# Tiled matmul groups issued in pairs, values loaded ahead of queries, and new plan times in an attention and MoE kernel

## The chip, the core and the metric

The kernel runs on one core of one Trainium2 chip. The metric is the device time of one execution in microseconds (us); the time before is the median of three runs. TensorE (PE in the profile) multiplies matrices into PSUM; ScalarE (ACT) and VectorE (DVE) evacuate PSUM and do elementwise work; GpSimd (POOL) issues the loads here and SyncE (SP) the transposing DMAs and the stores.

## The reference

For each of 8 batches and 8 heads, 576 tokens with head dimension 64, and 32 packed queries p per head:

```
p_packed = softmax(p k^T / 8) v
out      = softmax(q p_packed^T / 8) p_packed
x = out, heads side by side: 4608 tokens x 512
h = x @ w_in                 (512 x 2048)
g = h where h >= 1, 0 where h <= -1, else (h + 1)^2 / 4
result = g @ w_out           (2048 x 512)
```

## The kernel before, in words

The kernel folds the packed values into the first weight matrix: M = p_packed times the head's rows of w_in (`mk`, lines 472 to 483), so that the hidden layer is M times the second softmax A. A batch has these tasks, each a group of matmuls on TensorE followed by evacuations:

- `trans` (351): k and q, 96 tokens by 128, are transposed in two parts each (kT0, kT1, qT0, qT1). In batches 0 to 2 TensorE does it, and ScalarE or VectorE copies the result out (tile `tp`; in batch 0 as two copies). From batch 3 on (`TURNED`) a DMA of SyncE does it (`turned`, 485).
- `scores` (378): sc0 and sc1, 12 matmuls of 64 columns each, into one PSUM tile `sp`; ScalarE takes the exponential into `ex`.
- `packed` (397): exp times values, and the row sums (tile `pk`, shown as pk); a copy, an add and a copy make `ppT`, a reciprocal makes `rs`.
- `weights` (432), for two groups g of four heads: s2 (tile `s2`, shown as s in the profile, line 439), an exponential on ScalarE (`eT`), sm (sums over keys by a matmul with a block of ones), a logarithm (`ln`) and an exponential (`rc`) on ScalarE for the reciprocal, and the product `A` on VectorE.
- `mk` (472), for four quarters f of the 2048 hidden features: tile `mp`, cast into `M` by ScalarE or VectorE.
- `hidden_tile` (512), 16 per batch: h = M times A, 4 matmuls of 288 columns (line 519), then x on ScalarE (line 524), a second step on either engine (529 or 531), and hT on VectorE (534).
- `out_tile` (555), 9 for each pair of batches: 16 matmuls of 512 columns (line 562) into `o`, a copy to `ob` (line 307) and stores.

s2 and mp are tiled: each of their eight matmuls uses 64 rows and 32 columns of the array, so that the eight lie side by side. All other matmuls use the whole array. Group g of the heads before is h = 2a + g for a in 0 to 3, so each group needs both halves of qT.

PSUM has three wide tiles (`psW`, `NW`=3, of two banks each), used in turn by all tasks but the output tiles, and two output tiles (`psO`). Until the first outputs run, TensorE is kept busy by matmuls on zeros (line 624).

The order on every engine is static. `Plan` simulates the engines with the costs in `C` and emits the instructions in the order that it finds. Each task has a key (its priority), dependences, a PSUM room that it `takes`, and tasks that free the room again. `ready` says when a task can start, `choose` picks by time and key, `run` advances the clocks. `switch` is what it adds whenever TensorE goes between tiled and whole (`mode`), `land` what a DMA takes after its transfer, `xt` and `xland` the time and delay of a transposing DMA. Loads go through GpSimd's queue in the order in which `add_load` and `add_weights` are called: k, q and v of batch 0, w_in and w_out in quarters by turns, k, q and v of batch 1, then p.

Of the kernel before, what the change touches and what calls it, by code (L numbers as in the profile page):

```python
# [11 lines left out]
C = dict(load=3.0, w_in=2.65, w_out=2.55, out=9.0, p=3.1, land=1.9, xt=5.0, xland=2.5,  # L12
         tpp=0.06, tp=0.042, sc=0.034, pk=1.05, s2=0.25, sm=0.245, M=0.345, h=0.49, o=0.217, switch=0.05,
         pTc=0.1, Tca=1.12, Tcd=0.76, Tc2a=0.64, Tc2d=0.457, ex=0.82, ppT=0.42, ppo=0.41, ppa=0.4, ppd=0.2, rs=0.18, eT=0.74, ln=0.65, rc=0.68, A=0.82,
# [7 lines left out]
class Task:  # L22

    def __init__(self, engines, cost, key, deps, fn, takes, readers, frees, mode, slack, after, holds):
        self.engines, self.cost, self.key, self.deps, self.fn = engines, cost, key, list(deps), fn
        self.takes, self.readers, self.frees, self.mode = takes, readers, frees, mode
        self.slack, self.after, self.holds = slack, after, holds
        self.users, self.end, self.slot, self.gone = [], None, None, 0.0


class Plan:
# [24 lines left out]
    def ready(self, t, e):  # L56
        at = 0.0
        for d in t.deps:
            if e == "PE":
                lag = 0.0 if d.on == "PE" else C["feed"] + (C["margin"] if t.slack is None else t.slack)  # L60
            else:
                lag = C["array"] if d.on == "PE" else C["tell"] if d.on != e else 0.0
            at = max(at, d.end + lag)
        if t.takes:
            room = self.rooms[t.takes][self.count[t.takes] % len(self.rooms[t.takes])]
            if room is None:
                return None
            at = max(at, room + (C["feed"] if e == "PE" else 0.0))
        return at
# [39 lines left out]
    def run(self, idle):  # L109
# [10 lines left out]
        n = len(self.tasks)  # L120
        while n:
# [24 lines left out]
            if t.takes:  # L146
                room = self.rooms[t.takes]
                t.slot = self.count[t.takes] % len(room)
                room[t.slot] = None
                self.count[t.takes] += 1  # L150
                if t.readers == 0:
                    room[t.slot] = t.end + t.holds
            if t.frees is not None:
                f = t.frees
                f.gone = max(f.gone, t.end)
                f.readers -= 1
                if f.readers == 0:
                    self.rooms[f.takes][f.slot] = f.gone
# [17 lines left out]
def kernel(  # L176
# [95 lines left out]
    def add_load(nm, b, parts=1, deps=()):  # L272
        for i, hs in enumerate([ALL] if parts == 1 else HS):
            L[nm, b, i] = add(DMA, C["load"] / parts, -1, deps, lambda nm=nm, b=b, hs=hs: load(nm, b, hs))
        if parts == 1:
            L[nm, b, 1] = L[nm, b, 0]
# [62 lines left out]

    def attention(b, key):  # L340
# [9 lines left out]
        def trans(nm, i, dst, prev):  # L350
            box, ky = {}, key[nm + "T" + str(i)]

            def mm():
                tp = box["tp"] = wide([P, X, 1024], bf16, "tp")
                for j in range(X):
                    for h2 in range(2):
                        for e in range(E):
                            o = (h2 * E + e) * TP
                            nc.tensor.transpose(tp[:, j, o:o + TP],  # L359
                                                tok[nm, b][:, 4 * i + 2 * j + h2, X * e:X * (e + 1)].rearrange("p c d -> p (c d)"),  # L360
                                                ident[:TP, :TP])
            split = 2 if b == 0 else 1
            t = add(PE, C["tp"] * 12, ky, [L[nm, b, i]] + prev, mm, takes="W", readers=split, mode=0)
            if split == 1:
                def cp(eng):
                    w = 4 * E * TP
                    copy(dst()[:, i, :w].rearrange("p (j c) -> p j c", j=X), box["tp"][:, :, :w // 2])(eng)
                return t, [both(cp, C["Tca"], C["Tcd"], ky, [t], frees=t)]
            res = []
            for j in range(X):  # L370
                def cp(eng, j=j):
                    w = 2 * E * TP
                    copy(dst()[:, i, j * w:(j + 1) * w], box["tp"][:, j, :w])(eng)
                res.append(both(cp, C["Tc2a"], C["Tc2d"], ky, [t], frees=t))
            return t, res

        def scores(i, deps):
            box, ky = {}, key["sc" + str(i)]

            def mm():  # L380
                sp = box["sp"] = wide([P, 2, FW], f32, "sp")
                for j in range(2):
                    for e in range(E):
                        for g in range(G):
                            h, o = G * (2 * i + j) + g, (e * G + g) * X * NP
                            w = ((G * j + g) * E + e) * TP
                            nc.tensor.matmul(sp[:, j, o:o + X * NP], kT()[:, i, w:w + P],  # L387
                                             pT[:, b, h].rearrange("p x n -> p (x n)"), start=True, stop=True)

            def ev(eng):  # L390
                nc.scalar.activation(ex().rearrange("p e g x a n -> p a (e g x) n")[:, 2 * i:2 * i + 2],  # L391
                                     box["sp"][:TP, :, :E * G * X * NP].rearrange("p j (c n) -> p j c n", n=NP),
                                     AF.Exp, scale=scale)
            t = add(PE, C["sc"] * 12, ky, deps, mm, takes="W", readers=1, mode=0)
            return t, add(ACT, C["ex"], ky, [t] + old("pk"), ev, frees=t)

        def packed(deps):
            box, ky = {}, key["pk"]

            def mm():  # L400
# [3 lines left out]
                for g in range(G):  # L404
                    for a in range(Q):
                        h = G * a + g
# [9 lines left out]
            t = add(PE, C["pk"], ky, [L["v", b, 0]] + deps, mm, takes="W", readers=3, mode=0)  # L416
# [15 lines left out]
        def weights(g, deps, r):  # L432
            box, ky, km = {}, key["s2" + str(g)], key["sm" + str(g)]

            def mm():
                s2 = box["s2"] = wide([P, X, FW], f32, "s2")
                for a in range(Q):
                    for x in range(X):
                        nc.tensor.matmul(s2[a * NP:(a + 1) * NP, x, :HALF], pp_of(x, G * a + g),  # L439
                                         qT()[x * D:(x + 1) * D, a // 2, (G * (a % 2) + g) * E * TP:][:, :E * TP], start=True, stop=True)  # L440
# [21 lines left out]
            t = add(PE, C["s2"], ky, deps, mm, takes="W", readers=1, mode=2)  # L462
            e_ = add(ACT, C["eT"], ky, [t, r] + p_, exp2, frees=t)
# [6 lines left out]
            return t, e_, a_  # L470

        def mk(f, deps):
            box, ky = {}, key["M" + str(f)]

            def mm():
                mp = box["mp"] = wide([P, G, FW], f32, "mp")
                for a in range(Q):
                    for g in range(G):
                        nc.tensor.matmul(mp[a * NP:(a + 1) * NP, g], pp_of(g, G * a + g),  # L479
                                         w_in_sb[g * D:(g + 1) * D, a, f * FW:(f + 1) * FW], start=True, stop=True)  # L480
            t = add(PE, C["M"], ky, deps + [L["in", f]], mm, takes="W", readers=1, mode=2)
            return t, both(lambda eng: copy(M()[:, :, f * FW:(f + 1) * FW], box["mp"])(eng),
                           C["Mca"], C["Mcd"], ky, [t] + K.get((b - 2, "h"), []), frees=t)
# [19 lines left out]
        ws = [weights(g, pc + qc0 + qc1, r) for g in range(G)]  # L503
        ms = [mk(f, pc) for f in range(NF)]
# [50 lines left out]
    def out_tile(pr, i):  # L555
        box, prev = {}, []
        bs = range(2 * pr + i * P // S, 2 * pr + ((i + 1) * P - 1) // S + 1)

        def step(fi):
            if fi == 0:  # L560
                box["o"] = psO.tile([P, d_model], f32, tag="o", name="o")
            nc.tensor.matmul(box["o"], hT[:, fi, i * P:(i + 1) * P], w_out_sb[:, fi, :], start=(fi == 0), stop=(fi == KF - 1))  # L562
# [7 lines left out]
        def done_last(eng):  # L570

            w = d_model // 2
            for j, (eng, queue) in enumerate(((ACT, nc.scalar), (DVE, nc.sync))):
                ob = ops.tile([P, w], f32, tag="ob" + str(j), name="ob" + str(j), bufs=1)
                copy(ob, box["o"][:, j * w:(j + 1) * w])(eng)
                for a, n, dst in out_rows(pr, i):
                    queue.dma_start(dst[:, j * w:(j + 1) * w], ob[a:a + n])
        for fi in range(KF):
# [6 lines left out]
        both(done if 2 * pr + 2 < B or i + 1 < NT else done_last, C["oba"], C["obd"], b_key(pr, i), prev, frees=owner, takes="ob", holds=C["out"])  # L585
# [16 lines left out]
    order = "kT0 qT0 kT1 sc0 qT1 sc1 pk s20 M0 s21 sm0 M1 sm1 M2 M3".split()  # L602
# [52 lines left out]
```

## Time and profile before

| | us |
|---|---|
| median of 3 runs | 260.59 |
| lowest and highest | 259.56, 261.15 |
| the profiled execution, own time | 259.97 |
| its span, first to last instruction | 258.1 |
| TensorE busy | 248.6 |
| ScalarE busy | 189.5 |
| VectorE busy | 176.1 |

A row of the profile reads: start, duration, engine, line, operation, output<-input, shape, count. In a row of groups the numbers behind the bar are the total busy time, the mean of one in ns, and the idle time before with what ended it. Square brackets give an idle time and its releaser. Matmuls are pipelined, so the row of a matmul is longer than its distance to the next: distances between starts tell the cost.

### The profile page before, as it was taken

To read this page: it belongs to the slowest core of one execution; us is meant where nothing else is said; L and a number is where in the kernel's file an instruction comes from. 1 tells how busy PE (TensorE), PEld (TensorE's weight loads), DVE (VectorE), ACT (ScalarE), POOL (GpSimd) and SP (SyncE) were. 2 spreads that over 40 slices of the span, in tenths; PEclk is the share of its full clock that TensorE was granted. 3 is DMA by queue.
4 is the path that set the end of the run, shared out by engine and by line. 5 is a ranking of instruction groups with operands and counts; after the bars stand their busy time and mean duration, and the time that the engine had idled before them with its cause. 6 is when DMAs were issued, how large, how long until landed. Compare 5 with 4: busy or idle time off the path is not lost.

```text
span 258.1 us, 5590 instructions
## 1 busy us (share of the span) xinstructions
PE 248.6 (96%) x2273; PEld 145.2 (56%) x2273; DVE 176.1 (68%) x298; ACT 189.5 (73%) x304; POOL 27.4 (11%) x40
## 2 busy tenths in 40 slices
PE   7999999899999999999999999999999999999992
PEld 5977556357646645654655556555654465644440
DVE  5124997678899988999858885888367877940000
ACT  3438995789899799989869987998669885841110
POOL 8522312102101201110201000000000000000000
PEclk9999999999999999999999999999999999999998
DMA  7999999999999999999999994312021111132223
GB/s 100 181 207 207 206 205 194 218 228 209 164 177 165 164 218 195 166 156 144 181 138 159 214 221 89 79 30 54 4 80 41 43 41 42 43 81 82 60 64 83
DMA packets 54762, 34.38 MB, mean 133 GB/s; under 512 B 27472, under 2 KB 50256, under 8 KB 54736
## 3 DMA queue, kind: packets, MB, share of 16 engines
q0 software_dynamic: 24608, 18.55, 51.0%
q1 hardware_dynamic: 29968, 15.34, 33.8%
q8 instruction: 18, 0.29, 0.4%
q10 hardware_dynamic: 160, 0.13, 0.2%
q14 instruction: 8, 0.07, 0.1%
HBM read 37.22 MB, written 9.44 MB: 181 GB/s over the span
## 4 chain that ended last, share of the span: by engine, by line
PE 76%; DMA 15%; ACT 3%; POOL 2%; issue 1%; DVE 1%; POOLq 0%
PE o L562 45%; PE h L519 21%; DMA p_nat<-in_p_dram 8%; DMA w_out_sb<-in_moe_w_out_dram 7%; PE mp L479 3%; PE sp L387 2%; PE pk L408 2%; PE sm L449 1%; PE s L439 1%; ACT M L307 1%; PE tp L359 1%; PE pk L414 1%; ACT pT L307 1%; POOL w_in_sb L280 1%; ACT eT L444 1%
## 5 line engine op out<-in xcount | busy, mean ns | idle before, releaser
L562 PE MATMUL o<-w_out_sb,hT 128*128 128x512 bf16 x576 | 144.5, 379 | 0.7 <-ACT ob L307 0.5
L534 DVE SCALAR_TENSOR_TENSOR hT<-x 128x576 bf16<-128x576 f32 x128 | 93.3, 754 | 14.0 <-PE o L562 9.8
L562 PEld LDWEIGHTS <-hT 128*128 128x128 bf16 x576 | 54.5, 98 | 56.4 <-issue 5.0
L524 ACT ACTIVATE x<-h 128x576 f32<-128x576 f32 x128 | 78.4, 656 | 9.9 <-PE h L519 6.6
L519 PE MATMUL h<-A,M 128*128 128x288 bf16 x512 | 77.8, 286 | 0.3 <-ACT M L307 0.3
L519 PEld LDWEIGHTS <-M 128*128 128x128 bf16 x512 | 48.4, 98 | 24.7 <-issue 3.0
L529 DVE TENSOR_SCALAR x<-x 128x576 f32<-128x576 f32 x80 | 36.7, 459 | 16.9 <-ACT x L524 16.2
L307 ACT COPY ob<-o 128x512 f32<-128x512 f32 (+1 forms) x22 | 12.7, 577 | 30.8 <-PE o L562 30.7
L531 ACT ACTIVATE x<-x 128x576 f32<-128x576 f32 x48 | 32.1, 683 | 0.7
L307 DVE COPY ob<-o 128x512 f32<-128x512 f32 (+1 forms) x15 | 10.1, 673 | 26.6 <-ACT ob L307 24.9
L307 ACT CAST M<-mp 128x1024 bf16<-128x1024 f32 x20 | 19.9, 1008 | 1.2 <-PE mp L479 1.1
L624 PE MATMUL o<-zeros 128*128 128x256 bf16 x137 | 18.9, 285 | 1.2 <-DVE zeros L242 1.2
L307 DVE CAST M<-mp 128x1024 bf16<-128x1024 f32 x12 | 14.6, 1220 | 1.7 <-PE mp L479 1.6
L624 PEld LDWEIGHTS <-zeros 128*128 128x128 bf16 x137 | 13.4, 102 | 3.5 <-DVE zeros L242 1.2
L460 DVE SCALAR_TENSOR_TENSOR A<-eT,rs,rc 128x576 bf16<-128x576 bf16 x16 | 13.0, 814 | 2.7 <-ACT rc L457 2.6
L391 ACT ACTIVATE ex<-sp 96x768 bf16<-96x768 f32 x16 | 12.9, 814 | 2.0 <-PE sp L387 2.0
L254 POOL DMA_DIRECT2D k<-in_k_dram x9 | 7.3, 812 | 65.9 <-issue 28.0
L444 ACT ACTIVATE eT<-s,rs 128x576 bf16<-128x576 f32 x16 | 11.7, 743 | 2.9 <-PE s L439 2.8
L479 PE MATMUL mp<-w_in_sb,ppT 64*32 64x512 bf16 x256 | 13.1, 384 | 0.5 <-ACT x L524 0.5
L453 ACT ACTIVATE ln<-sm 128x576 f32<-128x576 f32 x16 | 10.5, 655 | 1.6 <-PE sm L449 1.4
L457 ACT ACTIVATE rc<-ln 128x576 f32<-128x576 f32 x16 | 10.9, 683 | 0.5
L387 PEld LDWEIGHTS <-kT 128*128 128x128 bf16 x192 | 7.8, 98 | 2.2 <-ACT kT L307 0.2
(47 smaller groups left out, 114.1 us busy)
## 6 DMA issues: line engine op xcount, KB each, us to landing
q<-in_q_dram POOLq DMA_DIRECT2D x8, 576.0 KB, 14.5
v<-in_v_dram POOLq DMA_DIRECT2D x8, 576.0 KB, 15.0
out_dram<-ob SPq DMA_DIRECT2D x23, 192.0 KB, 3.0
k<-in_k_dram POOLq DMA_DIRECT2D x7, 576.0 KB, 14.1
out_dram<-ob SPq DMA_DIRECT2D x24, 128.0 KB, 2.4
w_in_sb<-in_moe_w_in_dram POOLq DMA_DIRECT2D x4, 512.0 KB, 18.3
w_out_sb<-in_moe_w_out_dram POOLq DMA_DIRECT2D x4, 512.0 KB, 19.0
out_dram<-ob SPq DMA_DIRECT2D x23, 64.0 KB, 2.6
```

What stands on the lines that cost most here:

```text
L307: return lambda eng: nc.vector.tensor_copy(out_, in_) if eng == DVE else nc.scalar.copy(out_, in_)
L387: nc.tensor.matmul(sp[:, j, o:o + X * NP], kT()[:, i, w:w + P], pT[:, b, h].rearrange("p x n -> p (x n)"), start=True, stop=True)
L444: nc.scalar.activation(box["eT"], box["s2"][:, :, :HALF], AF.Exp, scale=rs()[:, g, 1:])
L460: nc.vector.scalar_tensor_tensor(A()[:, g], box["eT"], rs()[:, g, :1], box["rc"], ALU.mult, ALU.mult)
L479: nc.tensor.matmul(mp[a * NP:(a + 1) * NP, g], pp_of(g, G * a + g), w_in_sb[g * D:(g + 1) * D, a, f * FW:(f + 1) * FW], start=True, stop=True)
L519: nc.tensor.matmul(h[:, hf, :HALF], T[b, "M"][:, g, fi * P:(fi + 1) * P], T[b, "A"][:, g, hf], start=(g == 0), stop=(g == G - 1))
L524: nc.scalar.activation(box["x"], box["h"][:, :, :HALF], AF.Prelu, bias=-1.0, alpha=0.5)
L529: nc.vector.tensor_scalar(x, x, 1.0, 0.0, ALU.add, ALU.max)
L531: nc.scalar.activation(x, x, AF.Relu, bias=1.0)
L534: nc.vector.scalar_tensor_tensor(hT[:, fi, col:col + S].rearrange("p (a t) -> p a t", a=2), box["x"], 1.0, box["x"], ALU.min, ALU.mult)
L562: nc.tensor.matmul(box["o"], hT[:, fi, i * P:(i + 1) * P], w_out_sb[:, fi, :], start=(fi == 0), stop=(fi == KF - 1))
L624: plan.run(lambda: nc.tensor.matmul(o[:, :DW], zeros[:, :P], zeros[:, :DW], start=True, stop=True))
```

## The change

- From batch 2 on, s2 of group 0 goes with mp 0, s2 of group 1 with mp 1, and mp 2 with mp 3: each pair is one task of TensorE that takes two wide PSUM tiles. `weights` and `mk` become generators, and `tiled` runs one or two of them. A task can hold several rooms (`slots`, `readers` as a list).
- Head group g is now h = 4g + (a xor g): a half of the heads, so s2 of group g needs qT of half g alone, and the scores task i fills group i. Each score matmul writes its two runs of 32 columns 128 apart, and `ex` is written in one contiguous run per third.
- In batch 0, v is loaded ahead of q, and q in two halves; the copies of kT and qT are one instead of two.
- The last output tile accumulates in two PSUM tiles of 256 columns (one of them a wide one), so each half has its own copy engine; the longer store goes first.
- The plan: `first`=3.8 for the first v and q, `xland` 6.0 for 2.5, `switch` 0.09 on entering tiled work alone, `join` 0.11 off for a pair, `lap` 0.085 by which ScalarE and VectorE overlap successive instructions, the first cast of M on VectorE, more dependences for TensorE's tasks (old readers of `ex`, `ppT`, `A`, `M`), and from batch 1 on both kT ahead of qT.

The diff, cut to its core:

```diff
-C = dict(load=3.0, w_in=2.65, ..., xt=5.0, xland=2.5, ... switch=0.05,
+C = dict(load=3.0, first=3.8, w_in=2.65, ..., xt=5.0, xland=6.0, ... switch=0.09, lap=0.085, join=0.11,
...
         if t.takes:
-            room = self.rooms[t.takes][self.count[t.takes] % len(self.rooms[t.takes])]
-            if room is None:
-                return None
-            at = max(at, room + (C["feed"] if e == "PE" else 0.0))
+            rooms = self.rooms[t.takes]
+            for j in range(len(t.readers)):
+                room = rooms[(self.count[t.takes] + j) % len(rooms)]
+                if room is None:
+                    return None
+                at = max(at, room + (C["feed"] if e == "PE" else 0.0))
...
-                cost += C["switch"]
+                cost += C["switch"] if t.mode else 0.0
                 self.mode = t.mode
-            self.now[e] = at + cost
+            self.now[e] = at + cost - (C["lap"] if e in ("ACT", "DVE") and cost > 0.4 else 0.0)
...
     def first_loads():
         for hs in HS:
             load("k", 0, hs)
+        load("v", 0, ALL)
         make_identity(nc, ident)
...
-    add_load("q", 0)
-    add_load("v", 0)
+    L["v", 0, 0] = L["v", 0, 1] = add(DMA, C["first"], -1, (), lambda: None)
+    add_load("q", 0, 2, cost="first")
...
+    def head(g, a):
+        return 4 * g + (a ^ g)
...
-            split = 2 if b == 0 else 1
...
-                sp = box["sp"] = wide([P, 2, FW], f32, "sp")
-                for j in range(2):
-                    for e in range(E):
-                        for g in range(G):
-                            h, o = G * (2 * i + j) + g, (e * G + g) * X * NP
-                            w = ((G * j + g) * E + e) * TP
-                            nc.tensor.matmul(sp[:, j, o:o + X * NP], kT()[:, i, w:w + P],
-                                             pT[:, b, h].rearrange("p x n -> p (x n)"), start=True, stop=True)
+                sp = wide([P, 1024], f32, "sp")
+                box["sp"] = sp[:TP, :E * X * Q * NP].rearrange("p (e y) -> p e y", e=E)
+                for e in range(E):
+                    o = sp[:, e * X * Q * NP:(e + 1) * X * Q * NP].rearrange("p (x a n) -> p x a n", x=X, a=Q)
+                    for a in range(Q):
+                        h = head(i, a)
+                        w = (h % 4 * E + e) * TP
+                        nc.tensor.matmul(o[:, :, a], kT()[:, i, w:w + P], pT[:, b, h], start=True, stop=True)
...
-                        nc.tensor.matmul(s2[a * NP:(a + 1) * NP, x, :HALF], pp_of(x, G * a + g),
-                                         qT()[x * D:(x + 1) * D, a // 2, (G * (a % 2) + g) * E * TP:][:, :E * TP], start=True, stop=True)
+                        nc.tensor.matmul(s2[a * NP:(a + 1) * NP, x, :HALF], pp_of(x, h),
+                                         qT()[x * D:(x + 1) * D, g, h % 4 * E * TP:][:, :E * TP], start=True, stop=True)
...
-            t = add(PE, C["s2"], ky, deps, mm, takes="W", readers=1, mode=2)
+            t, j = yield ky, C["s2"], deps + p_, mm
...
+        def tiled(*units):
+            units = list(units)
+            asked = [next(u) for u in units]
+            t = add(PE, sum(a[1] for a in asked) - C["join"] * (len(asked) - 1), asked[0][0], [d for a in asked for d in a[2]],
+                    lambda: [a[3]() for a in asked], takes="W", readers=[1] * len(units), mode=2)
+            return [u.send((t, j)) for j, u in enumerate(units)]
...
-        ws = [weights(g, pc + qc0 + qc1, r) for g in range(G)]
-        ms = [mk(f, pc) for f in range(NF)]
+        ws, ms = [weights(g, pc + (qc0, qc1)[g], r) for g in range(G)], [mk(f, pc) for f in range(NF)]
+        if b < 2:
+            ws, ms = [tiled(w)[0] for w in ws], [tiled(m)[0] for m in ms]
+        else:
+            pairs = [tiled(w, m) for w, m in zip(ws, ms)] + [tiled(*ms[2:])]
+            ws, ms = [p_[0] for p_ in pairs[:2]], [p_[1] for p_ in pairs[:2]] + pairs[2]
...
-            nc.tensor.matmul(box["o"], hT[:, fi, i * P:(i + 1) * P], w_out_sb[:, fi, :], start=(fi == 0), stop=(fi == KF - 1))
+            for o, cs in [(box["o"][:, :w], slice(w)), (box["o2"], slice(w, d_model))] if end else [(box["o"], slice(d_model))]:
+                nc.tensor.matmul(o, hT[:, fi, i * P:(i + 1) * P], w_out_sb[:, fi, cs], start=(fi == 0), stop=(fi == KF - 1))
...
-            for j, (eng, queue) in enumerate(((ACT, nc.scalar), (DVE, nc.sync))):
+            for j, (eng, queue, o) in enumerate(((ACT, nc.scalar, box["o"][:, :w]), (DVE, nc.sync, box["o2"]))):
                 ob = ops.tile([P, w], f32, tag="ob" + str(j), name="ob" + str(j), bufs=1)
-                copy(ob, box["o"][:, j * w:(j + 1) * w])(eng)
-                for a, n, dst in out_rows(pr, i):
+                copy(ob, o)(eng)
+                for a, n, dst in sorted(out_rows(pr, i), key=lambda x: -x[1]):
...
-    order = "kT0 qT0 kT1 sc0 qT1 sc1 pk s20 M0 s21 sm0 M1 sm1 M2 M3".split()
+    order = "kT0 kT1 sc0 qT0 sc1 qT1 pk s20 M0 s21 sm0 M1 sm1 M2 M3".split()
```

More of the change, by code (lines that the diff above doesn't have):

```diff
@@ L8 @@
 from concourse._compat import with_exitstack
-C = dict(load=3.0, w_in=2.65, w_out=2.55, out=9.0, p=3.1, land=1.9, xt=5.0, xland=2.5,
-         tpp=0.06, tp=0.042, sc=0.034, pk=1.05, s2=0.25, sm=0.245, M=0.345, h=0.49, o=0.217, switch=0.05,
-         pTc=0.1, Tca=1.12, Tcd=0.76, Tc2a=0.64, Tc2d=0.457, ex=0.82, ppT=0.42, ppo=0.41, ppa=0.4, ppd=0.2, rs=0.18, eT=0.74, ln=0.65, rc=0.68, A=0.82,
+C = dict(load=3.0, first=3.8, w_in=2.65, w_out=2.55, out=9.0, p=3.1, land=1.9, xt=5.0, xland=6.0,
+         tpp=0.06, tp=0.042, sc=0.034, pk=1.05, s2=0.25, sm=0.245, M=0.345, h=0.49, o=0.217, switch=0.09, lap=0.085, join=0.11,
+         pTc=0.1, Tca=1.12, Tcd=0.76, ex=0.82, ppT=0.42, ppo=0.41, ppa=0.4, ppd=0.2, rs=0.18, eT=0.74, ln=0.65, rc=0.68, A=0.82,
          Mca=1.0, Mcd=1.22, x=0.65, ta=0.683, td=0.457, hT=0.758, oba=0.585, obd=0.69,
@@ L25, in __init__ @@
         self.engines, self.cost, self.key, self.deps, self.fn = engines, cost, key, list(deps), fn
[L26 to L28 removed]
+        self.takes, self.readers = takes, list(readers) if isinstance(readers, (list, tuple)) else [readers]
+        self.frees = (frees, 0) if isinstance(frees, Task) else frees
+        self.mode, self.slack, self.after, self.holds = mode, slack, after, holds
+        self.users, self.end, self.slots, self.gone = [], None, None, [0.0] * len(self.readers)
 class Plan:
@@ L147, in run @@
                 room = self.rooms[t.takes]
[L148 to L152, printed above, removed]
-            if t.frees is not None:
[L154 to L158, printed above, removed]
+                t.slots = [(self.count[t.takes] + j) % len(room) for j in range(len(t.readers))]
+                self.count[t.takes] += len(t.slots)
+                for n_, j in zip(t.readers, t.slots):
+                    room[j] = None if n_ else t.end + t.holds
+            if t.frees is not None:
+                f, j = t.frees
+                f.gone[j] = max(f.gone[j], t.end)
+                f.readers[j] -= 1
+                if f.readers[j] == 0:
+                    self.rooms[f.takes][f.slots[j]] = f.gone[j]
             if len(t.engines) > 1:
@@ L270, with add_load @@
     L = {}
-    def add_load(nm, b, parts=1, deps=()):
+    def add_load(nm, b, parts=1, deps=(), cost="load"):
         for i, hs in enumerate([ALL] if parts == 1 else HS):
-            L[nm, b, i] = add(DMA, C["load"] / parts, -1, deps, lambda nm=nm, b=b, hs=hs: load(nm, b, hs))
+            L[nm, b, i] = add(DMA, C[cost] / parts, -1, deps, lambda nm=nm, b=b, hs=hs: load(nm, b, hs))
         if parts == 1:
@@ L361, in mm, with cp @@
                                                 ident[:TP, :TP])
-            split = 2 if b == 0 else 1
[L363 to L375, printed above, removed]
+            t = add(PE, C["tp"] * 12, ky, [L[nm, b, i]] + prev, mm, takes="W", readers=1, mode=0)
+            def cp(eng):
+                w = 4 * E * TP
+                copy(dst()[:, i, :w].rearrange("p (j c) -> p j c", j=X), box["tp"][:, :, :w // 2])(eng)
+            return t, [both(cp, C["Tca"], C["Tcd"], ky, [t], frees=t)]
         def scores(i, deps):
@@ L478, in mm @@
                     for g in range(G):
[L479 to L483, printed above, removed]
+                        h = head(g, a)
+                        y = h % 2
+                        nc.tensor.matmul(mp[a * NP:(a + 1) * NP, g], pp_of(y, h),
+                                         w_in_sb[y * D:(y + 1) * D, h // 2, f * FW:(f + 1) * FW], start=True, stop=True)
+            t, j = yield ky, C["M"], deps + [L["in", f]] + K.get((b - 2, "h"), []), mm
+            cp = lambda eng: copy(M()[:, :, f * FW:(f + 1) * FW], box["mp"])(eng)
+            war = K.get((b - 2, "h"), [])
+            if (b, f) == (0, 0):
+                yield t, add(DVE, C["Mcd"], ky, [t], cp, frees=(t, j))
+            yield t, both(cp, C["Mca"], C["Mcd"], ky, [t] + war, frees=(t, j))
+        def tiled(*units):
[4 more added lines that the diff above has]
+            return [u.send((t, j)) for j, u in enumerate(units)]
         def turned(nm, i, dst, prev):
@@ L557, in out_tile, with spare @@
         bs = range(2 * pr + i * P // S, 2 * pr + ((i + 1) * P - 1) // S + 1)
+        end = 2 * pr + 2 == B and i + 1 == NT
+        w = d_model // 2
+        def spare():
+            box["o2"] = wide([P, w], f32, "o2")
         def step(fi):
@@ L584, in out_tile @@
                 owner = t
-        both(done if 2 * pr + 2 < B or i + 1 < NT else done_last, C["oba"], C["obd"], b_key(pr, i), prev, frees=owner, takes="ob", holds=C["out"])
+        both(done_last if end else done, C["oba"], C["obd"], b_key(pr, i), prev, frees=owner, takes="ob", holds=C["out"])
     def b_key(pr, i):
```

18 lines of the change are left out of this document (9 added, 9 removed).

## The prediction

> **What bounds the kernel now.** I read the page first, then busy times by stage, then TensorE's instructions in order of time with the waits of its weight loads, and last the three places that the change touches: start, tiled groups, end.
>
> ```profile
> span 258.1 us, 5590 instructions
> PE 248.6 (96%) x2273; PEld 145.2 (56%) x2273; DVE 176.1 (68%) x298; ACT 189.5 (73%) x304; POOL 27.4 (11%) x40
> ```
>
> 96% names TensorE, but the stages differ:
>
> ```profile
> 23.60:44.40 20.80, 19.70 (x198) 12.33 (x191) 17.88 (x29) 17.54 (x28) 5.24 (x7) 1.00 1.34 202
> 44.40:55.50 11.10, 10.27 (x122) 4.76 (x123) 7.26 (x10) 8.48 (x13) 0.77 (x1) 1.00 1.29 224
> 55.50:77.70 22.20, 21.66 (x254) 13.52 (x253) 19.03 (x33) 20.33 (x32) 2.58 (x3) 1.00 1.33 186
> ...
> 102.10:125.00 22.90, 22.90 (x227) 13.50 (x226) 21.20 (x37) 21.05 (x34) 2.48 (x4) 1.00 1.31 161
> ...
> 223.64 29.73 PE L562 MATMUL o<-w_out_sb,hT 128*128 128x512 bf16 x137
> ```
>
> (After the stretch: its length, then busy us of TensorE, weight loads, VectorE, ScalarE, GpSimd; clock, DMA share, GB/s. The granted clock is full.) In the last stretch shown, and from about 80 us on, TensorE has no gap that another engine makes, and 137 output matmuls stand ready behind the last hidden tile: a reserve of 29.6 us. There, what TensorE is spared comes off the end, and a delay on ScalarE or VectorE only uses up reserve. Up to 78 us it is otherwise: ScalarE works 20.33 of 22.20 us, VectorE 19.03, and only two output tiles can be open, so their matmuls fill no more than the hidden tiles allow. There a gain must come from loads, evacuations and order.
>
> **The tiled matmuls in pairs.** A group of s (line 439) or mp (line 479) is eight matmuls on 64x32 tiles, side by side. The order of time in batch 5, and one place in batch 4:
>
> ```profile
> 137.10 2.75 PE L562 MATMUL o<-w_out_sb,hT 128*128 128x512 bf16 x12
> 139.78 0.32 PE L439 MATMUL s<-qT,ppT 64*32 64x288 bf16 x8
> 139.92 0.40 PE L479 MATMUL mp<-w_in_sb,ppT 64*32 64x512 bf16 x8
> 140.25 0.67 PE L519 MATMUL h<-A,M 128*128 128x288 bf16 x4
> 140.75 0.38 PE L562 MATMUL o<-w_out_sb,hT 128*128 128x512 bf16 x1
> 141.06 0.32 PE L439 MATMUL s<-qT,ppT 64*32 64x288 bf16 x8
> 141.31 0.82 PE L562 MATMUL o<-w_out_sb,hT 128*128 128x512 bf16 x3
> 141.97 0.65 PE L519 MATMUL h<-A,M 128*128 128x288 bf16 x4
> ...
> 143.93 0.41 PE L479 MATMUL mp<-w_in_sb,ppT 64*32 64x512 bf16 x8
> 144.27 0.39 PE L562 MATMUL o<-w_out_sb,hT 128*128 128x512 bf16 x1
> ```
> ```profile
> 114.87 0.40 PE L479 MATMUL mp<-w_in_sb,ppT 64*32 64x512 bf16 x8
> 115.09 0.31 PE L439 MATMUL s<-qT,ppT 64*32 64x288 bf16 x8
> ```
>
> Durations overlap, so go by starts. Three o take 0.66 us (141.31 to 141.97): 0.22 each. An o ahead of a tiled group holds it off 0.31 (140.75 to 141.06): 0.09 to enter. s alone then takes 0.25, mp alone 0.34 to the next start. Two groups alone cost 0.09 + 0.25 + 0.09 + 0.34 = 0.77. The pair at 139.78 costs 0.14 + 0.33 and one entry: 0.56. A join is worth 0.21. Two mp in a row are not in the trace; the nearest is mp followed by s, 0.22 to the next start against 0.34 to an untiled one, and with the entry this is 0.21 again. Bounds 0.09 (the entry alone) and 0.43 (the second group free beside the first); I take 0.21.
>
> [...]
>
> How many joins? The waits of the weight loads from 80 to 224 us, the time of batches 3 to 7, tell how many islands of tiled work there are:
>
> ```profile
> PEld L479 <- issue: 4.5, 16, 0.4
> PEld L439 <- issue: 3.1, 8, 0.4
> PEld L439 <- DVE rs L426: 0.4, 1, 0.4
> ```
>
> Each row but the last counts gaps that no engine made; the last is one entry whose s also waited for a scale. 25 islands for 30 groups (six a batch); five are joined by chance already. The change makes three a batch, 15. Ten joins: **-2.1 us**, on the path. [...] Batch 2 falls from six islands to three, 0.63, but there TensorE is not alone the bound: half, **-0.3**.
>
> What the pair adds: it takes two of the three wide PSUM buffers at once. Untiled work in front of it must be evacuated twice.
>
> ```profile
> L524 ACT ACTIVATE x<-h 128x576 f32<-128x576 f32 x128 | 78.4, 656 | 9.9 <-PE h L519 6.6 <-DVE hT L534 2.7
> 76.94 0.41 PE L479 MATMUL mp<-w_in_sb,ppT 64*32 64x512 bf16 x8 [0.53 <-ACT x L524]
> ```
>
> Queued behind a waiting pair is all of TensorE, and behind that ScalarE, which lives from h. Bounds per pair: 0 (the planner asks for both buffers and places o in between) and one more evacuation, 0.66. The only such wait in the page of waits is the 0.53 quoted, one among 32 mp groups; 18 pairs at that rate give 18/32 x 0.53: **+0.3**.
>
> **Values ahead of queries, heads by halves.** The rows of the start (GpSimd waits name the landing of a load) and of the two chains:
>
> ```profile
> 11.75 0.75 POOL L280 DMA_DIRECT2D w_in_sb<-in_moe_w_in_dram  x1 [2.42 <-DMA q<-in_q_dram]
> 15.87 0.74 POOL L282 DMA_DIRECT2D w_out_sb<-in_moe_w_out_dram  x1 [3.37 <-DMA v<-in_v_dram]
> 18.06 0.79 POOL L254 DMA_DIRECT2D k<-in_k_dram  x1 [1.45 <-DMA w_in_sb<-in_moe_w_in_dram]
> ...
> 15.63 0.87 PE L408 MATMUL pk<-ex,v 96*128 96x64 bf16 x24 [0.36 <-DMA v<-in_v_dram]
> 18.26 0.44 PE L439 MATMUL s<-qT,ppT 64*32 64x288 bf16 x16
> 23.64 1.15 PE L519 MATMUL h<-A,M 128*128 128x288 bf16 x8
> 44.36 0.87 PE L408 MATMUL pk<-ex,v 96*128 96x64 bf16 x24 [0.38 <-DMA v<-in_v_dram]
> 55.47 0.65 PE L519 MATMUL h<-A,M 128*128 128x288 bf16 x4
> ...
> 21.31 0.82 DVE L460 SCALAR_TENSOR_TENSOR A<-eT,rs,rc 128x576 bf16<-128x576 bf16 x1 [1.10 <-ACT rc L457]
> ```
>
> Now q lands at about 11.7, v at 15.6, pk waits for v, and s follows pk by 2.6 us. With the places exchanged v lands at 11.7 and pk starts by about 12.2, so its results are there by 14.8; the second half of q lands at 15.6. Its transposes, copy and hand-overs I put at 1.7 us (an estimate, at two thirds of the 2.63 us from pk to s, which has four such steps): s of the second half at 17.3, of the first some 1.5 us earlier. Today both halves have s at 18.26 and the second queues behind the first on ScalarE: 5.4 us to the first h. The first half, with nothing ahead of it, has its A from 21.31 on, for 0.82: with the hand-over 4.0 us after s. With the halves apart the second has that path too: first h at 17.3 + 4.0 = 21.3, 2.3 us earlier. What is late then is the second half of q, and after it w_in. Bounds: 0 (M0 must wait for w_in, whose place is the same, 18.06; with its matmuls and cast it is done by about 20) and 2.6 (all that lies between pk and s).
>
> Does it reach the end? Loads are unchanged in sum, so v of batch 1 lands at 44.4 as before, and its chain begins there. In between ScalarE and VectorE work 17.5 and 17.9 of 20.8 us; 2.3 us more room drains them sooner, and o that stood after 44.4 comes before it. From pk to the first h batch 1 takes 11.1 us, batch 0 took 8.0: the 3.1 us over are copies queued ahead of the chain, which the drained engines can give back. I take two thirds: **-2.1**; bounds 0 (the landing of v decides alone) and -3.1 plus the gaps of 55.5 to 77.7, 0.5: -3.6.
>
> Steps costed at nothing, with their cover: one more issue on GpSimd (0.75 in the rows) ahead of the weights, while those already issued fill the DMA; without that cover 0.75 on the first h. The identity is made one issue later. Copies of kT and qT in batch 0 as one instead of two: hidden behind the landing of v. The planner's transposes landing later, its laps and the added dependences move order only: no row of before shows a TensorE wait on them beyond 80 us; uncovered, they are the stalls of the second rival.
>
> **The last tile.** ScalarE and VectorE read halves of one tile, one after the other:
>
> ```profile
> 253.41 0.37 ACT L307 COPY ob<-o 128x256 f32<-128x256 f32 x1 [2.82 <-PE o L562]
> 253.82 0.86 ACTq L577 DMA_DIRECT2D out_dram<-ob  x2
> 253.82 0.42 DVE L307 COPY ob<-o 128x256 f32<-128x256 f32 x1 [24.86 <-ACT ob L307]
> 254.27 0.82 SPq L577 DMA_DIRECT2D out_dram<-ob  x2
> 20.36 3.00 PE L624 MATMUL o<-zeros 128*128 128x256 bf16 x26
> ```
>
> With two tiles VectorE starts at 253.4, and SyncE's stores 0.4 earlier: -0.4. Longest store first: 0 to -0.4 (one issue), taken at -0.2. The 32 half-width matmuls at 3.00/26 = 0.115 take 3.7 us against 16 x 0.22 = 3.5: +0.2 at most, taken at +0.1. Together **-0.5**.
>
> Sum: -2.1 - 0.3 + 0.3 - 2.1 - 0.5 = -4.7. The profiled execution took 259.97 us (span 258.1), 0.6 under the median of 260.59; 259.97 becomes 255.3, and the median **255.9 us**.
>
> **The rivals.** *The start is hidden:* for it speaks that batch 1 waits for its own v at 44.36, whatever happened before; against it the 3.1 us of excess behind that wait. Then -4.7 + 2.1 = -2.6: 258.0 us.
>
> *Pairs starve evacuation (the other side):* each of 18 pairs holds two of three wide buffers while TensorE waits for the second. At 0.66 each this is 11.9 in place of 0.3: 255.9 + 11.6 = 267.5 us. It makes the kernel slower by 1% from (263.2 - 255.6)/18 = 0.42 us a pair. For it: the 0.53 at 76.94, and ScalarE at 92% there. Against it: one such wait among 32, and from 80 us on o to put in between. [...]
>
> *Scores written in pieces:* each score matmul now writes two runs of 32 columns, 128 apart, where it wrote 64 in a row.
>
> ```profile
> 157.79 0.51 PE L387 MATMUL sp<-pT,kT 128*128 128x64 bf16 x12
> 158.14 0.38 PE L562 MATMUL o<-w_out_sb,hT 128*128 128x512 bf16 x1
> ```
>
> Twelve take 0.35 us (157.79 to 158.14). Twice that for all 16 groups is +5.6: 261.5 us. No row shows such a write; I take nothing. [...]
>
> **How the numbers follow.** A measurement of this kernel tells about 1% from no change: 258.0 to 263.2. Forecast 0.58, between 253.2 and 257.9, all faster; better than that 0.05, faster; start hidden 0.20, around 258.0, 0.05 of it faster and 0.15 same; starving pairs 0.13, 0.03 same and 0.10 slower; scores 0.04, same 0.03 and slower 0.01. So faster 0.68, same 0.21, slower 0.11. The range goes from 252.8 (both bounds of start and tail) to 260.0, which leaves out the slower cases and a little at the bottom.
>
> **What would show it.** Right: 15 islands instead of 25 after the start of batch 3, each of about 0.56 to 0.65 us; pk of batch 0 near 12.2, first h near 21.3, first h of batch 1 near 53.4; VectorE's last copy beside ScalarE's. Wrong: TensorE waits on x or M ahead of pairs; batch 1 starting its h at 55.5 again; score groups of over 0.4 us; gaps of TensorE past 80 us, which the order of before does not have.

## The result and the profile after

The changed kernel takes 262.58 us (median of 11 runs, 260.84 to 264.13) against 259.56 for the kernel before, measured beside it: ratio 1.0108, 95% interval 1.0083 to 1.0134. It is slower by 1%, where 255.9 was forecast (4.7 less than the 260.59 of the three runs that stand under Time and profile before). The profiled execution is the slowest of the eleven, 264.13 us with a span of 262.4; that of before had 258.1. So 4.3 us of span are to be found, against 3.0 between the medians: the profiled execution ran at a mean granted clock of 0.990, the other ten at 0.996 to 1.000, so the slow stretch shown next, about 1.2 us, is this execution's alone.

The page after:

```profile
span 262.4 us, 5578 instructions
PE 247.7 (94%) x2254; PEld 146.6 (56%) x2287; DVE 178.3 (68%) x304; ACT 181.2 (69%) x294; POOL 27.9 (11%) x41
PEclk9999999999999997999999999999999999999998
```

TensorE's share falls from 96% to 94%, and in slice 16 its clock is down. Three stretches around that slice (columns as before: length, busy us by engine, clock):

```profile
85.00:95.00 10.00, 9.72 (x85) 5.17 (x84) 8.18 (x14) 9.64 (x17) 1.14 (x2) 1.00 1.34 184
95.00:105.00 10.00, 7.00 (x93) 4.22 (x94) 7.08 (x13) 5.69 (x10) 0.77 (x1) 0.83 1.32 206
105.00:115.00 10.00, 9.82 (x76) 5.89 (x76) 8.01 (x14) 7.52 (x14) 2.46 (x3) 1.00 1.25 208
```

TensorE lost 3 us there, and the mean clock of those 10 us was 0.83. Its order of time names the cause:

```profile
95.43 0.51 PE L390 MATMUL sp<-pT,kT 128*128 128x64 bf16 x12
98.88 0.52 PE L390 MATMUL sp<-pT,kT 128*128 128x64 bf16 x12 [2.94 <-DMA kT<-k]
...
101.47 1.49 PE L408 MATMUL pk<-ex,v 96*128 96x64 bf16 x24
102.77 0.49 PE L414 MATMUL pk<-ones,ex 96*128 96x2 bf16 x12
...
122.71 0.86 PE L408 MATMUL pk<-ex,v 96*128 96x64 bf16 x24
123.41 0.44 PE L414 MATMUL pk<-ones,ex 96*128 96x2 bf16 x12
```

The second scores of batch 4 wait 2.94 us for a transposing DMA. Behind that wait pk takes 1.30 us to its next row (101.47 to 102.77) where another batch takes 0.70: half speed for a while (a granted clock of 0.50 from 100.07 to 103.48), about 1.2 us in sum over the rows from 99 to 107 (an estimate, against the same rows elsewhere). Before, the same scores stood far later, behind a transpose of nearly the same time (SyncE's issue of the second kT of batch 4, then the scores; first before, then after):

```profile
87.62 4.02 SPq L487 DMA_TRANSPOSE kT<-k  x1
107.60 0.51 PE L387 MATMUL sp<-pT,kT 128*128 128x64 bf16 x12
```
```profile
85.40 2.86 SPq L501 DMA_TRANSPOSE kT<-k  x1
```

20 us lay between issue and use, and the landing took 14.2 of them; now it is 10.5 to where TensorE begins to wait, and the landing took 13.4. The plan reckons 11.0 (`xt` 5.0 and `xland` 6.0).

The second loss is spread out. Runs of hidden tiles, after and then before:

```profile
92.01 1.74 PE L537 MATMUL h<-A,M 128*128 128x288 bf16 x12
109.73 4.79 PE L537 MATMUL h<-A,M 128*128 128x288 bf16 x34
...
147.14 1.19 PE L537 MATMUL h<-A,M 128*128 128x288 bf16 x8
```
```profile
90.59 1.14 PE L519 MATMUL h<-A,M 128*128 128x288 bf16 x8
102.10 1.63 PE L519 MATMUL h<-A,M 128*128 128x288 bf16 x12
```

Eight took 1.14 and take 1.19, twelve took 1.63 and take 1.74: TensorE waits some 0.05 us ahead of every tile. Such a gap stands in no list of waits. I take it from the starts of the matmuls: the distance to the next start less what the first one costs (0.122 for h, 0.216 for o), counted where h is next and the rest is 0.03 to 0.2 us. After: 43 such gaps, 3.3 us; before: 5, 0.6 us (the expectations below name 3.5 and 0.7 for them).

The start moved, and lost it again in batch 1 (TensorE's order of time, then ScalarE's and VectorE's):

```profile
12.69 0.87 PE L408 MATMUL pk<-ex,v 96*128 96x64 bf16 x24
16.26 0.32 PE L440 MATMUL s<-qT,ppT 64*32 64x288 bf16 x8
18.25 0.32 PE L440 MATMUL s<-qT,ppT 64*32 64x288 bf16 x8
22.58 1.63 PE L537 MATMUL h<-A,M 128*128 128x288 bf16 x12
...
49.78 0.32 PE L440 MATMUL s<-qT,ppT 64*32 64x288 bf16 x8 [1.60 <-ACT pT L312]
55.50 0.65 PE L537 MATMUL h<-A,M 128*128 128x288 bf16 x4
```
```profile
46.72 1.59 ACT L312 COPY pT<-tpp 64x768 bf16<-64x768 bf16 x2
48.94 0.80 ACT L312 COPY pT<-tpp 64x768 bf16<-64x768 bf16 x1 [0.62 <-DVE pT L312]
```
```profile
48.34 0.56 DVE L312 COPY pT<-tpp 64x768 bf16<-64x768 bf16 x1 [0.88 <-ACT pT L312]
```

pk is 2.9 us earlier, the first h 1.1, the first h of batch 1 not at all (55.47 before). Four copies read one wide tile in turn for 3 us, and the second s of batch 1 needs that tile.

The pairs did as forecast. First the waits of the weight loads from 86 to 224 us (us in total, times, longest), then two rows of TensorE's order of time:

```profile
PEld L440 <- issue: 4.1, 10, 0.5
PEld L482 <- issue: 2.2, 6, 0.4
```
```profile
207.26 0.63 PE L482 MATMUL mp<-w_in_sb,ppT 64*32 64x512 bf16 x16
207.82 0.42 PE L450 MATMUL sm<-eT,onesblk 128*128 128x288 bf16 x2
```

16 islands, one of them the last of batch 2, so 15 for batches 3 to 7 in place of 25. Two mp in a row, which the trace before did not have, take 0.56 to the next start, 0.65 with the entry, against 0.86 for two alone: 0.21 saved.

The end after, where both copies run side by side:

```profile
257.90 0.37 ACT L312 COPY ob<-o 128x256 f32<-128x256 f32 x1 [2.75 <-PE o L587]
258.01 0.42 DVE L312 COPY ob<-o 128x256 f32<-128x256 f32 x1 [25.60 <-PE o L587]
258.46 0.79 SPq L601 DMA_DIRECT2D out_dram<-ob  x2
```

From ScalarE's last copy to the end of the span: 4.46 us, before 4.69. Together, as a rough account of this execution: 12 islands fewer in the whole kernel (28 for 40) -2.5, the late transpose and the slow clock +4.1, gaps ahead of h +2.8, the wait of s in batch 1 +1.3 (1.60 and, before, 0.27 of another wait on the same copies), first h -1.1, end -0.2: +4.4 for the 4.3.

### The profile page after: what moved, and what is told of

Read it like the earlier page. It is cut to its first block, busy times and chain, and to the rows that moved or that the text cites. A ratio compares the mean times of both kernels' runs of the same rounds, so it can differ in the third digit from the quotient of the medians.

```text
span 262.4 us, 5578 instructions
## 1 busy us (share of the span) xinstructions
PE 247.7 (94%) x2254; PEld 146.6 (56%) x2287; DVE 178.3 (68%) x304; ACT 181.2 (69%) x294; POOL 27.9 (11%) x41
## 4 chain that ended last, share of the span: by engine, by line
PE 74%; DVE 13%; DMA 5%; ACT 4%; issue 3%; ACTq 0%
PE o L587 40%; PE h L537 17%; DVE hT L552 6%; PE o L650 5%; DMA kT<-k 5%; PE mp L482 3%; DVE x L547 2%; PE pk L408 2%; ACT x L542 2%; PE tp L369 2%; PE sp L390 2%; PE sm L450 1%; PE s L440 1%; DVE ob L312 1%; ACT pT L312 1%
## 5 line engine op out<-in xcount | busy, mean ns | idle before, releaser
L587 PE MATMUL o<-w_out_sb,hT 128*128 128x512 bf16 (+1 forms) x559 | 132.8, 374 | 1.8 <-issue 0.5
L542 ACT ACTIVATE x<-h 128x576 f32<-128x576 f32 x128 | 76.5, 654 | 8.0 <-PE h L537 5.3
L537 PE MATMUL h<-A,M 128*128 128x288 bf16 x512 | 74.7, 285 | 1.7 <-ACT x L542 0.8
L547 DVE TENSOR_SCALAR x<-x 128x576 f32<-128x576 f32 x85 | 38.7, 456 | 8.9 <-ACT x L542 7.9
L312 ACT COPY ob<-o 128x512 f32<-128x512 f32 (+1 forms) x25 | 14.4, 576 | 39.3 <-PE o L587 38.8
L549 ACT ACTIVATE x<-x 128x576 f32<-128x576 f32 x43 | 28.9, 686 | 0.4
L312 DVE COPY ob<-o 128x512 f32<-128x512 f32 (+1 forms) x12 | 8.0, 666 | 30.7 <-PE o L587 25.6
L312 DVE CAST M<-mp 128x1024 bf16<-128x1024 f32 x15 | 18.3, 1222 | 7.9 <-PE mp L482 7.9
L312 ACT CAST M<-mp 128x1024 bf16<-128x1024 f32 x17 | 16.9, 1010 | 3.5 <-PE mp L482 3.5
L454 ACT ACTIVATE ln<-sm 128x576 f32<-128x576 f32 x16 | 10.5, 656 | 2.7 <-PE sm L450 2.6
L390 PE MATMUL sp<-pT,kT 128*128 128x64 bf16 x192 | 8.2, 193 | 3.1 <-DMA kT<-k 2.9
## 6 DMA issues: line engine op xcount, KB each, us to landing
w_in_sb<-in_moe_w_in_dram POOLq DMA_DIRECT2D x4, 512.0 KB, 17.3
```

What stands on the lines that cost most here:

```text
L312: return lambda eng: nc.vector.tensor_copy(out_, in_) if eng == DVE else nc.scalar.copy(out_, in_)
L390: nc.tensor.matmul(o[:, :, a], kT()[:, i, w:w + P], pT[:, b, h], start=True, stop=True)
L537: nc.tensor.matmul(h[:, hf, :HALF], T[b, "M"][:, g, fi * P:(fi + 1) * P], T[b, "A"][:, g, hf], start=(g == 0), stop=(g == G - 1))
L542: nc.scalar.activation(box["x"], box["h"][:, :, :HALF], AF.Prelu, bias=-1.0, alpha=0.5)
L547: nc.vector.tensor_scalar(x, x, 1.0, 0.0, ALU.add, ALU.max)
L549: nc.scalar.activation(x, x, AF.Relu, bias=1.0)
```

## The experiments

The runs were made on three chips. The kernel before took 259.75 us beside e1 to e4, 259.84 beside e5 to e8, 259.76 beside e9 to e11 and 260.06 beside e12, and each ratio is against the figure beside it.

Theory 1: the planner's new times make its plan too tight in two places. `choose` lets a task of higher priority go first if TensorE idles for it less than `wait` x the cost of the task that could start at once. With an o of 0.217 and `wait` 0.5 that is 0.109 us. A tile's first step on ScalarE counted 0.65 against 0.49 for its matmuls, 0.16 of waiting, so an o was put in between. With the lap it counts 0.565: 0.075 of waiting, and TensorE is made to wait. And with faster evacuations the plan brings scores 10 us forward, while the transposes come hardly faster (in batch 4 14.2 us to landing before, 13.4 after). Theory 2: the late transposes alone. Theory 3: pairs hold two of three wide tiles and starve the evacuation, the forecast's rival.

**e1, no laps.**

```diff
-... switch=0.09, lap=0.085, join=0.11,
+... switch=0.09, lap=0.0, join=0.11,
```

> The changed kernel with lap = 0 alone: the planner lets ScalarE and VectorE start the next instruction only when the one before has ended, as before. Theory 1 (the laps make the planner run too tight: it lets TensorE wait a little for nearly every hidden tile, where it placed an output matmul, and puts the scores of batch 4 ahead of their transposes): both go, 3 to 5 us less than the changed kernel, 257.5 to 259.5, no TensorE wait on kT over 1 us, gaps ahead of h rarer. Theory 2 (only the late transposes of kT and the clock that drops behind that wait): 258 to 259 if the scores come after their transposes, with the small gaps ahead of h still there. Theory 3 (pairs hold two of three wide buffers and starve the evacuation): unchanged, 262 or more.

Median 261.82, with times from 256.9 to 264.06; one execution, the profiled one, ran at a granted clock of 0.56 throughout and took 422.87. The ratio 0.9953 (0.9907 to 0.9998) counts only the four executions nearest the fastest one, so it flatters. The two at a granted clock of 1.0 took 256.9 and 257.26 us, the other seven, at 0.985 to 0.992, 260.11 to 264.06. Inconclusive by itself; e12 reads it.

**e2, later landings in the plan.**

```diff
-C = dict(load=3.0, ..., xt=5.0, xland=6.0,
+C = dict(load=3.0, ..., xt=5.0, xland=12.0,
```

> The changed kernel with xland = 12 for 6 alone: the planner reckons with transposes that land later, so it puts the scores of batch 4 later; laps and pairs stay. Theory 1: the 3 us wait on kT and the lower clock behind it go, the small gaps ahead of h stay: 259 to 260.5. Theory 2: all of the loss goes, 256 to 258.5. Theory 3: unchanged, 262 or more.

260.82 us, ratio 1.0039 (1.0022 to 1.0056), its times within 260.46 and 262.32. No wait on kT; the gaps ahead of h stay, 39 with 3.2 us. The time is 0.3 above theory 1's range, whose signs are there; theory 2 falls, as the kernel is still slower than before.

**e3, a stricter choice.**

```diff
-... margin=0.15, wait=0.5)
+... margin=0.15, wait=0.2)
```

> The changed kernel with wait = 0.2 for 0.5 alone: the planner prefers a task of higher key only when TensorE waits for it less than a fifth of the cost of the task that could start at once. Theory 1: the small gaps ahead of h go (some 3 us), the wait on kT may stay, as the scores are planned early again: 258 to 260. Theory 2: unchanged, 261 to 264, with the wait on kT. Theory 3: unchanged, 262 or more.

260.01 us, ratio 0.999 (0.9963 to 1.0017), at the upper end of theory 1's range. The gaps ahead of h are gone (6, 0.5 us), the transposes are late again, now in batch 3:

```profile
79.11 0.82 PE L390 MATMUL sp<-pT,kT 128*128 128x64 bf16 x12 [2.84 <-DMA kT<-k]
```

**e4, single tasks.**

```diff
-        if b < 2:
+        if b < B:
```

> The changed kernel with no pairs: s2 and mp are single tasks in all batches, everything else as changed. Theory 1 and 2: the joins are lost (12 islands at 0.21 = 2.5 us), the wait on kT depends on where the scores go: 261 to 265. Theory 3: the starvation goes and the kernel is faster than the changed one, 258 to 260.

262.85 us, ratio 1.0092 (1.0064 to 1.0121): not the 258 to 260 of theory 3. But the order differs, and another wait came, for qT, so that e6 has to decide it:

```profile
PE s L440 <- DMA qT<-q: 2.8, 2, 1.9
```

It also shows what moves the scores. Without pairs those of batch 4 start at 100.41, with pairs at 95.43, and before at 104.98 (without and with pairs in e6 and e5: 103.64 and 96.45). So a part of the 10 us by which the scores came forward is the pairs', not the laps'.

**e5, both:** the edits of e2 and e3 together.

> The changed kernel with xland = 12 and wait = 0.2 together. Theory 1 (two separate losses of the planner's: scores ahead of their transposes, and small gaps ahead of h): both go and they add up, 257 to 258.5, under the kernel before. Theory 2 (the late transposes alone): as with xland = 12 alone, 260 to 261. Theory 3 (pairs starve the evacuation): 261 or more.

256.53 us, ratio 0.9878 (0.9857 to 0.9899), just under theory 1's range: the two losses are separate and both of the planner's. The 6.0 us under the changed kernel are more than the 1.8 of e2 and the 2.6 of e3 together, as in e3 transposes were late again in another place. What TensorE still waits for in e5:

```profile
PE s L440 <- ACT pT L312: 1.4, 1, 1.4
PE o L650 <- DVE zeros L246: 1.2, 1, 1.2
PE o L587 <- DVE hT L552: 0.9, 2, 0.6
PE o L587 <- issue: 0.5, 3, 0.2
PE tpp L324 <- DVE p_nat L321: 0.4, 1, 0.4
```

No transpose is among them, and the gaps ahead of h are 5 with 0.4 us.

**e6, e5 without pairs:** the edits of e2, e3 and e4.

> The kernel of e5 without pairs, s2 and mp single in all batches. If a join is worth 0.21 also here, the 16 islands more in this order cost 3.4 us: 260.5 to 262. If pairs cost in evacuation what they save, the same as e5 within 1 us.

261.02 us, ratio 1.0038 (1.0025 to 1.0051). The pairs are worth 4.5 us between the medians, over the 3.4 of 16 islands (43 for 27); what the other 1.1 is, these runs don't tell. Theory 3 falls here: the pairs gain, and TensorE waits for no transpose in either kernel. And without pairs the kernel is 1.2 us slower than the one before, of which its three islands more (43 for 40) make 0.6: what start and end gain is lost elsewhere, and no run isolates where.

**e7, e5 with q ahead of v.**

```diff
-        load("v", 0, ALL)
...
-    L["v", 0, 0] = L["v", 0, 1] = add(DMA, C["first"], -1, (), lambda: None)
-    add_load("q", 0, 2, cost="first")
+    add_load("q", 0, cost="first")
+    add_load("v", 0, cost="first")
```

> The kernel of e5 with q of batch 0 loaded whole and ahead of v, at the same planned times for all later loads. If the earlier first h does not reach the end (batch 1 waits for its own v and its own chain), the same as e5 within 0.7 us though the first h is 1 to 2 us later. If it reaches the end as forecast, 1.5 to 2.5 us slower than e5.

257.53 us, ratio 0.9924 (0.9894 to 0.9954): 1.0 us slower than e5, between the two expectations. In the profiles the first h is 3 us later (25.73 against 22.75; 1.0 of it because k landed later in this execution), so a third to a half of what the change of place gives reaches the end, in an order with two islands fewer (25 for 27).

**e8, the kernel before with `wait=0.2`:** e3's edit, made in the kernel before.

> The kernel before with wait = 0.2 alone. Theory 1: the planner of before reckons ScalarE and VectorE too slow, so the gaps that it plans ahead of h are not on the chip (6 gaps, 0.7 us in its trace), and the rule changes little: 258.8 to 260. Other reading (the rule costs TensorE time whatever the laps): 3 to 4.5 us faster, 255 to 257.

259.24 us, ratio 0.9982 (0.9962 to 1.0001). Without laps the rule costs next to nothing, as theory 1 says.

**e9, e5 with the last tile in one PSUM tile.**

```diff
-            for o, cs in [(box["o"][:, :w], slice(w)), (box["o2"], slice(w, d_model))] if end else [(box["o"], slice(d_model))]:
+            for o, cs in [(box["o"], slice(d_model))]:
...
-            for j, (eng, queue, o) in enumerate(((ACT, nc.scalar, box["o"][:, :w]), (DVE, nc.sync, box["o2"]))):
+            for j, (eng, queue, o) in enumerate(((ACT, nc.scalar, box["o"][:, :w]), (DVE, nc.sync, box["o"][:, w:]))):
...
-                for a, n, dst in sorted(out_rows(pr, i), key=lambda x: -x[1]):
+                for a, n, dst in out_rows(pr, i):
...
-        if end:
-            prev = [add(PE, 0.0, 100 + pr * NT + i, [K[B - 1, "h"][-1]], spare, takes="W", readers=1)]
```

> The kernel of e5 with the last output tile in one PSUM tile and the stores in the old order; nothing else in the order of work differs. By the prediction's term (0.5 with bounds 0.2 and 0.8): 0.4 to 0.6 us slower than e5, with VectorE's last copy 0.4 us behind ScalarE's. If the stores hide it: the same.

256.92 us, ratio 0.9884 (0.9869 to 0.99), 0.4 slower between the medians but overlapping e5's interval. The profiles show what the times can't part:

```profile
251.58 0.37 ACT L312 COPY ob<-o 128x256 f32<-128x256 f32 x1 [2.82 <-PE o L587]
251.98 0.42 DVE L312 COPY ob<-o 128x256 f32<-128x256 f32 x1 [25.52 <-ACT ob L312]
```

From 251.58 to the end (256.3) 4.7 us; in e5 4.4. The term is 0.3.

**e10, e5 with p's transposes later.**

```diff
-            add_pT(PB, B, 0.9, [L["p"]], False)
+            add_pT(PB, B, 0.9, [L["p"]] + K[1, "s2"], False)
```

> The kernel of e5 with the transposes of p for batches 2 to 7 put behind both s2 of batch 1. In e5 the second s2 of batch 1 waits 1.5 us for the wide tile that these transposes hold while four copies read it in turn. If that wait is what keeps the earlier start from the end: 1 to 1.5 us faster than e5, first h of batch 1 earlier by as much. If the chain of batch 1 then waits for the same copies elsewhere: within 0.5 us of e5 or slower.

256.91 us, ratio 0.9897 (0.9879 to 0.9916): no gain. The wait moved to the first h of batch 1, behind the same copies:

```profile
57.85 1.69 PE L537 MATMUL h<-A,M 128*128 128x288 bf16 x12 [1.07 <-DVE pT L312]
```

**e11, e5 without laps:** the edits of e1, e2 and e3.

> The kernel of e5 with lap = 0. If the laps do harm by themselves, faster than e5 by over 1 us. By theory 1 they did harm only with wait = 0.5 and xland = 6, and here they are neutral or a gain: the same as e5 to 1.5 us slower, with no TensorE wait on kT.

255.85 us, ratio 0.9849 (0.9835 to 0.9862): 0.7 faster than e5 between the medians, though the intervals touch, a little better than expected and the fastest version of all, 1.5% under the kernel before. No wait on kT. Even here the laps gain nothing.

**e12, e1 once more,** the same edit.

> The kernel of e1 (the changed kernel with lap = 0 alone) once more, since its profiled execution ran at a granted clock of 0.56 throughout and its gaps can't be read. Theory 1: few small gaps ahead of h (under 1.5 us in sum, 3.5 in the changed kernel), since they come from laps and wait = 0.5 together, and waits on a transposed kT or qT of up to several us in some executions, which is what spreads its times from 257 to 264. If the gaps are there as before, the laps are not their cause.

263.5 us in the profiled execution, 265.39 in the other; ratio 1.0174 (1.0082 to 1.0266) from these two. Gaps ahead of h: 5, 0.5 us, so laps and `wait` make them together. And one wait that is longer than ever:

```profile
PE sp L390 <- DMA kT<-k: 5.1, 1, 5.1
```

So laps are not what puts scores ahead of their transposes, against what theory 1 expected of e1: here it is batch 6, whose scores start at 129.70, 155.82 before. This transpose landed 9.3 us after its issue, within the plan's 11.0, but TensorE wanted it 4.3 us after its issue at 120.32. With `xland` at 6 transposes are late with laps or without. The times spread over 3.0 to 7.2 us in the changed kernel, e1 (its longest left out), e3 and e4, and over 0.8 to 2.4 in the runs of the changed kernel with `xland` at 12. That late transposes make the spread fits this and the clocks of e1, but only the profiled executions show the waits.

## Why the prediction was wrong

The step that failed is the one costed at nothing: "The planner's transposes landing later, its laps and the added dependences move order only: no row of before shows a TensorE wait on them beyond 80 us". No wait in the rows of before could show it, as their order kept 14.6 us or more between the issue of a kT and its use (20 in batch 4), and an o ahead of nearly every h. But the landings of kT in the same trace could have shown the risk:

```profile
DMA to landing us min/median/max: 4.5/10.1/19.0
```

Against these the plan reckons 11.0 from issue to use (7.5 before the change). The change took the slack away. The o ahead of h went because laps and `wait` of 0.5 together let TensorE wait: either one taken back ends the gaps (e3, e12). The scores came nearer to their transposes through pairs (e4, e6), laps (batch 4 starts at 99.25 in e12) and perhaps through the rest of the new order, which no run takes apart. Put right, `xland` alone gives back 1.8 us (e2 against the changed kernel), `wait` alone 2.6 (e3), and both 6.0 (e5). The last "what would show it" named these signs, gaps past 80 us, but the prediction had them only as stalls of the pairs' rival, with no chance or price of their own.

That e5 and e11 end near the forecast 255.9 is in part luck. In e5 the pairs are worth 4.5 us against e6 where 2.1 net was forecast, the start about 1.0 for 2.1, the end 0.3 for 0.5, and something in the rest of the change costs some 2.5 us (e6 is 1.2 slower than the kernel before, in spite of the gains at start and end; 0.6 are its three islands more).

- Joins: right in kind and count (15 islands, one entry each), and 0.21 each for a second mp as well. -2.1 was if anything small; e6 gives 4.5 for all of them. What the prediction left out is that a pair also brings later scores forward (e4).
- Pairs starving the evacuation, the rival for the slower side: wrong (e6). The result was slower for another reason.
- Scores written in pieces: no price. Twelve take 0.35 us after, as they did before (157.79 to 158.14):

```profile
119.50 0.51 PE L390 MATMUL sp<-pT,kT 128*128 128x64 bf16 x12
119.85 0.38 PE L587 MATMUL o<-w_out_sb,hT 128*128 128x512 bf16 x1
```

- Start: too large. pk came at 12.69, near the forecast 12.2, s of the second half at 18.25 and not 17.3, the first h at 22.58 and not 21.3, since TensorE had q's second transposes behind the first s in its order and VectorE cast M ahead of the first A. Of the -2.1 e7 shows about -1.0; batch 1's chain waits for copies of pT that the price left out, and moving these copies only moves the wait (e10).
- The last tile: the size, -0.3 for -0.5.
- The range: its lower end, 252.8, does not follow from the bounds it names. Those of start and tail, 1.5 and 0.3 below the forecast, give 254.1.

## What to carry to other kernels

A planner's constants are part of the kernel. When some are made more exact, look at what the inexact ones had paid for: their slack may be the cover of waits that no list of waits shows, because they never happened. Price an order change by the distance from issue to use of every transfer that it brings nearer, against the longest landing in the trace and not the median.

## What the runs showed of the hardware

Behind a wait of TensorE of 2.94 us its clock was halved: in the profiled execution the clock granted is 0.50 for 3.41 us from 100.07 on, 1.2 us after the end of the wait, and this costs about 1.2 us on top of 2.9. In e3 the page has the clock at 7 tenths in the slice of 6.5 us in which the wait of 2.84 us ends. In e12 it has 7 and 6 tenths in the slice of the wait of 5.09 us and the one behind it, and the 11 o behind that wait take 0.43 us each (130.34 to 135.06), where three in the trace before took 0.22 each. In e4 the clock is 0.50 for 3.42 us behind a wait of 1.89 us (a stretch of the changed kernel, then the wait in e4 and the stretch behind it; in a stretch the clock is the number ahead of the last two):

```profile
100.07:103.48 3.41, 3.41 (x56) 2.18 (x56) 2.26 (x3) 1.68 (x4) 0.08 (x1) 0.50 1.19 217
```
```profile
110.03 0.32 PE L440 MATMUL s<-qT,ppT 64*32 64x288 bf16 x8 [1.89 <-DMA qT<-q]
```
```profile
111.32:114.74 3.42, 3.42 (x16) 0.98 (x15) 2.29 (x5) 2.62 (x4) 0.00 (x0) 0.50 1.82 94
```

e2, e5 and e11, whose longest waits after the start are 1.59, 1.38 and 1.06 us, have no such stretch: their pages have the clock at 9 tenths or more in every slice but the last, in which the last matmul ends. Where the border lies is not shown. In e3 the seven executions at a mean clock of 0.986 to 0.992 took 259.59 to 261.10 us, the three at 0.998 or more 258.12 to 258.43.
